# Splitting the first three hidden-layer matmul groups of token tile 0 in two along the contraction

## The chip, the cores and the metric

The kernel runs on one core of a Trainium2 chip. The metric is the time of one execution on the device, in microseconds. Every execution computes the whole reference from tensors in device memory and writes the whole output back.

## The reference

Two stages follow each other. The first is an attention over 8 batches, 8 heads, 576 positions and 64 channels, in two parts that are added; the second is a two-layer feed-forward block over 4608 tokens with an ELU between the layers.

```python
q_d, k_d, v_d = (mean over groups of 4 positions of q, k, v)      # 144 positions
out_d  = softmax(q_d @ k_d.T / 8) @ v_d                           # each row repeated 4 times
mask   = abs(pos[:, None] - pos[None, :]) < 4
out_local = softmax(where(mask, q @ k.T / 8, -1e9)) @ v
x = (repeat(out_d, 4) + out_local)        # [8*576, 8*64] = [4608, 512]
h = x @ w_in                              # w_in  [512, 2048]
g = where(h > 0, h, exp(min(h, 0)) - 1)
out = g @ w_out                           # w_out [2048, 512]
```

## The kernel before

**Pieces of work.** The attention goes batch by batch, and in a batch by pairs of heads (`j` = 0 to 3). A pair gives 128 channels of `x`, so that the four pairs are the four chunks of 128 over which the first layer's product is contracted. The feed-forward block goes by token tiles of 512 tokens (`t` = 0 to 8). Batch 0 holds tokens 0 to 575, and so all of tile 0 and the first 64 tokens of tile 1.

**Names.** Each piece is an operation with a name, an engine and a function that issues its instructions. With `b` the batch and `j` the pair: `tq`/`tk` (TensorE) turn q and k, `evq`/`evk` copy them out of PSUM, `sc` (TensorE) makes the scores, `ex` (ScalarE) is their exponential, `mask` (VectorE) applies the band where it isn't added on TensorE, `den` and `recip` give the denominators, `spr` (TensorE) and `evr` spread them, `out` (TensorE, 36 matmuls a pair) multiplies by v, `xn` (VectorE, L910 and L914) multiplies by the reciprocal, and `add` followed by batch, pair and tile (L933) adds the two parts and writes the pair's chunk of the tile buffer `xt`. In batch 0 `add000` and `add020` are GpSimd's, `add010` and `add030` VectorE's. `vc` (L572) casts a quarter of a batch's v on GpSimd after its loads `vm` on SyncE's queue have landed; `cast` (L625) casts q or k. `w0` to `w3` load quarters of `w_in`, `w4` to `w7` quarters of `w_out`, all on GpSimd's queue.

**The feed-forward block.** For tile `t` and each of 16 chunks `fc` of 128 hidden units, `mm1_t_fc` (L950) issues four matmuls of 128x512, one for each pair's chunk of `xt`, into one PSUM bank. `exp` (ScalarE, L956), `min` (VectorE, L958) and `elu` (VectorE, L961) follow; `elu` reads the bank for the last time. For each of the four groups of 128 tokens `tt`, the product with `w_out` is cut in four operations `mm2_t_tt0` to `mm2_t_tt3` (L979), each of four matmuls over four hidden chunks, in one bank; `os` (ScalarE, L995) copies it out and `st` stores it.

**What sets the order.** The program has no loop on the chip: a planner in Python writes the order out. Each operation has a rank (a due time from hand-set numbers) and an assumed duration; the planner plays the engines against each other with these, always starts the ready operation of lowest rank whose buffers are free, and keeps the order that comes out. Every engine then runs its own operations strictly in that order. A change of one operation's operands, rank or length can thus move operations that it never mentions.

**Banks.** PSUM has eight banks. While batches after the first are under way, banks 0 to 3 go to attention work in twos; banks 4 to 7 go to the first layer (`hp`, at most three at a time), the second layer (`op`, at most two) and single attention banks. Which operation gets which is settled by the planner too.

**Fillers.** Until a set time the planner puts a `fill` (L357), a matmul of 128x512 on zeros, on TensorE wherever it has nothing to do.

**Around the change.** The order on TensorE is: `spr02`, `spr03` (L841), four fills, `out02`, `out03` (L883), three fills, `tq10`, a fill, `tk10`, a fill, `mm1_0_0`, `sc10`, `tq11`, `mm1_0_1`, `tk11`, `mm1_0_2`, two fills, `sc11`, `mm1_0_3` and so on.

Of the kernel before, what the change touches and what calls it, by code (L numbers as in the profile page):

```python
# [28 lines left out]
FCN, DMC = DFF // 128, DM // 128  # L29
# [9 lines left out]
      "cast131", "vc10", "vc12")  # L39
LGATE = (None, "recip00", "evv00", "recip00", "recip02", "xn00", "xn01", "xn02", "xn03", "elu0_0", "elu0_2", "elu0_4", "elu0_8")  # L40
BY_PE = (0, 1)
WIC = (0, 512, 1024, 1536, 2048)


# [20 lines left out]
class Plan:  # L65
# [9 lines left out]
    def op(self, eng, dur, rank, fn, reads=(), writes=(), after=(), name="", nbytes=0, rate=1.0, packet=97):  # L75
        o = Op(eng, dur, rank, fn, name)
        o.nbytes, o.rate, o.packet = nbytes, rate, packet
        for b in list(reads) + list(writes):
            if b in reads or b.kind not in self.PARTS:
                o.pre.update(b.writers)  # L80
            if b not in o.bufs:
                o.bufs.append(b)
        o.pre.update(after)
        for b in writes:
            b.writers.append(o)
        for b in o.bufs:
            b.ops.append(o)
        self.ops.append(o)
        return o
# [173 lines left out]
    def emit(self):  # L263
        for o in self.order:
# [8 lines left out]
PARAM = dict(e_d0=2, e_d1=0, e_d2=0, e_d3=1, M0=27.21, P=36.34, LAG=0.71, LEAD=52.25, GAP=6.32, SC=5.0,  # L273
             DEN=30.8, OUT=1.3, OUTG=2.09, LOAD=15.53, VLOAD=34.45, VCAST=9.57, warm=3.4, FILL=36.0, WI=-28.49,
             WO=59.77, WOG=5.01, OVER=1.64, LEAD1=58.97, GAP1=6.47, OUT1=55.0, VLOAD1=29.88, LOAD1=41.47,
             CC=-34.39, tv0=-22.07, C0=-2, SC0=3.1, OUTA=-23.54, OUTB=-20, DEN0=2.92, DENB=-27.58, SPA=-26.75,
             SPB=-20.86, V0=-43, G0=0, G1=0, G2=0, G3=2, G4=12, G5=6, G6=12, G7=3, G8=13, L0=0, L1=1, L2=2,
             L3=4, L4=4, LAG0=0.75, BY4=-51.82, TV1=0.68, C1=-19.87, e_cq0=0, e_cq1=1, e_cq2=1, e_cq3=1,
             e_ck0=0, e_ck1=0, e_ck2=1, e_ck3=1, e_q0=1, e_q1=0, e_q2=0, e_q3=0, e_k0=1, e_k1=1, e_k2=0,
             e_k3=0, QG=2.5, tvA=-26, e_v0=2, e_v1=1, e_v2=2, e_v3=1, e_g0=1, e_g1=1, e_g2=1, e_g3=1, e_r0=1,  # L280
             e_r1=0, e_r2=1, e_r3=1, e_xr0=0, e_xr1=1, e_xr2=0, e_xr3=1, e_a0=1, e_a1=0, e_a2=1, e_a3=0,
# [18 lines left out]
def kernel(  # L300
# [42 lines left out]
    def at(b):  # L343
        return T[b.kind][b.slot[0]]
# [4 lines left out]
    def one(b, p0, p1, a, z):  # L349
        return PS[p0:p1, b.slot[0], a:z]  # L350

    plan = Plan(SLOTS, MOE_BANKS)
# [8 lines left out]
    op = plan.op  # L361
# [232 lines left out]
    wi_ops, wo_ops = {}, {}  # L594

    def weights(i):
        wi = i < 4
        if wi:
            lo, hi = WIC[i], WIC[i + 1]
            src = moe_w_in.rearrange("(c p) m -> p c m", p=128)[:, :, lo:hi]  # L600
# [96 lines left out]
    def pool_v(b):  # L697

        yv, zs, w = st[b], (Buf("two", b < EARLY), Buf("one")), Buf("vd")

        def tv():
            t = at(yv)
            for g in range(3):
                for i in range(4):
                    nc.tensor.matmul(  # L705
                        PS[32 * i : 32 * i + 32, zs[g // 2].slot[0] + g % 2, :], C["VR"][:],
                        t[:, :, :, 2 * g + i % 2, :], start=True, stop=True, tile_position=(0, 32 * i),
                    )

        st[b, "vd"] = w  # L710
        return yv, zs, w, tv
# [88 lines left out]
    def denominators(b, js):  # L800
# [25 lines left out]
        else:  # L826
            op("PE", 0.48, r, go, reads=list(xs.values()), writes=[z], after=[o_mark], name=f"den{b}{js[0]}").mode = "c32"
        op("DVE", 0.56, r + 0.2, lambda: nc.vector.reciprocal(out=at(c)[p0:p1], in_=one(z, p0, p1, 0, HD)),  # L828
           reads=[z], writes=[c], name=f"recip{b}{js[0]}")
        if b in BY_PE:  # L830
            if js[0] == 0:
# [72 lines left out]
    def normalize(b, j, z):  # L904
        r, y, w = out_rank(b, j), stR[b, j], Buf("xn")

        def go():
# [11 lines left out]

        op("DVE", 0.98, r + 0.2, go, reads=[z], writes=[w, y], after=[evr[b, j]] if b in BY_PE else y.writers,  # L920
           name=f"xn{b}{j}")
# [20 lines left out]
    def mm1(t, fc):  # L942
        r = M0 + P * t + P * fc / FCN
        if fc == 0:
            gts[t] = Buf("gt")
        h, e, x, gt = Buf("hp"), Buf("e"), xts[t], gts[t]

        def go(dcs):
            for dc in dcs:
                nc.tensor.matmul(  # L950
                    one(h, 0, 128, 0, TBLK), WI[:, dc, 128 * fc : 128 * fc + 128], at(x)[:, dc, :],
                    start=(dc == 0), stop=(dc == DMC - 1),
                )

        op("PE", 0.863, r, lambda: go(range(DMC)), reads=[x], writes=[h], after=[wi_ops[fc]], name=f"mm1_{t}_{fc}")
        op("ACT", 0.55, r, lambda: nc.scalar.activation(out=at(e)[:], in_=one(h, 0, 128, 0, TBLK), func=AF.Exp),  # L956
           reads=[h], writes=[e], name=f"exp{t}_{fc}")
        op("DVE", 0.42, r, lambda: nc.vector.tensor_scalar(  # L958
            out=at(e)[:], in0=at(e)[:], scalar1=1.0, scalar2=-1.0, op0=AB.min, op1=AB.add),
           reads=[e], writes=[e], name=f"min{t}_{fc}")  # L960
        op("DVE", 0.64, r, lambda: nc.vector.scalar_tensor_tensor(  # L961
            out=at(gt)[:, fc, :], in0=one(h, 0, 128, 0, TBLK), scalar=0.0, op0=AB.max, in1=at(e)[:], op1=AB.add),
           reads=[h, e], writes=[gt], name=f"elu{t}_{fc}")
# [36 lines left out]
    for b in range(B):  # L1000
# [16 lines left out]
        if b in DEN_GROUPS:  # L1017
            yv, zv, w, tv = pool_v(b)
# [9 lines left out]
    for t in range(NT):  # L1028
        for fc in range(FCN):
            mm1(t, fc)  # L1030
        for tt in range(4):
            mm2(t, tt)
# [63 lines left out]
```

## Time and profile before

| what | value |
|---|---|
| three timed runs | 349.20, 350.22, 355.65 us; median 350.22 |
| the profiled execution | 349.04 us |
| its span, first to last instruction | 347.3 us |
| TensorE busy | 331.9 us, 4672 matmuls |
| VectorE, ScalarE, GpSimd busy | 218.0, 196.4, 132.6 us |
| moved by DMA | 49.73 MB |

The profile is one execution. Its own time is 1.7 us more than its span, and 1.2 us under the median of the runs. "Idle before" is time in which an engine had nothing running, with what ended it; "issue" means that the profile shows nothing that the engine waited for. Busy time of TensorE counts matmuls of 128x512 as about 380 ns each although they start 216 ns apart when nothing is in the way, so distances between starts are used for costs.

### The profile page before, as it was taken

What the parts mean: (1) busy time and instruction counts of PE and PEld (TensorE: products, weight loads), DVE (VectorE), ACT (ScalarE), POOL (GpSimd) and SP (SyncE); (2) the same over time, 40 slices, a digit from 0 to 9 for tenths busy, and PEclk for the clock granted to TensorE, in tenths of its full rate; (3) what the DMA queues carried; (4) which work ended last, traced back from release to release, by engine and by line L of the source; (5) the groups of instructions that cost most, each with busy time, mean ns of one, the idle gap of its engine ahead of it and who ended that gap; (6) DMA issues with size and microseconds to landing.
All of it is one profiled execution on the core that took longest, in us unless ns stands there. A gap on an engine that the chain in (4) does not pass through costs nothing.

```text
span 347.3 us, 10965 instructions
## 1 busy us (share of the span) xinstructions
PE 331.9 (96%) x4672; PEld 172.4 (50%) x4672; DVE 218.0 (63%) x459; ACT 196.4 (57%) x337; POOL 132.6 (38%) x190
## 2 busy tenths in 40 slices
PE   6967999999999999899989999999999999999995
PEld 3744564555554455445544455545554444444443
DVE  6564788467474986377756786577657738655530
ACT  3582577297754686277817762776376325444431
POOL 6583133765449443732455246623410150000000
PEclk9896999999999999999999999999999999999999
DMA  8999999999999999999957995003100310001011
GB/s 204 208 213 243 195 191 205 176 192 233 223 186 202 237 227 224 178 244 216 192 131 141 189 202 137 32 32 87 64 32 30 90 64 30 32 30 60 32 54 67
DMA packets 120196, 49.73 MB, mean 143 GB/s; under 512 B 106996, under 2 KB 114708, under 8 KB 120148
## 3 DMA queue, kind: packets, MB, share of 16 engines
q1 hardware_dynamic: 112004, 39.33, 58.1%
q0 software_dynamic: 6592, 9.32, 14.5%
q8 instruction: 36, 0.59, 0.8%
q10 hardware_dynamic: 1552, 0.39, 0.6%
q14 instruction: 12, 0.10, 0.1%
HBM read 44.27 MB, written 9.55 MB: 155 GB/s over the span
## 4 chain that ended last, share of the span: by engine, by line
PE 58%; issue 0%; ACT 0%; DVE 0%; ACTq 0%
PE bank L979 27%; PE bank L950 24%; PE bank L662 2%; PE bank L883 2%; PE bank L757 1%; PE bank L705 1%; PE bank L810 1%; ACT os L995 0%; DVE xn L914 0%; ACTq L995 0%
## 5 line engine op out<-in xcount | busy, mean ns | idle before, releaser
L979 PE MATMUL bank<-WO,gt 128*128 128x512 f16 (+1 forms) x592 | 141.5, 374 | 1.5 <-DVE xn L914 1.2
L950 PE MATMUL bank<-xt,WI 128*128 128x512 f16 x576 | 141.6, 380 | 0.5 <-DVE gt L961 0.5
L956 ACT ACTIVATE e<-bank 128x512 f16<-128x512 f32 x144 | 86.8, 604 | 62.0 <-PE bank L950 45.1
L958 DVE TENSOR_SCALAR e<-e 128x512 f16<-128x512 f16 x144 | 58.0, 406 | 72.7 <-ACT e L956 72.5
L961 DVE SCALAR_TENSOR_TENSOR gt<-bank,e 128x512 f16<-128x512 f32 x144 | 98.6, 689 | 5.2
L979 PEld LDWEIGHTS <-gt 128*128 128x128 f16 x592 | 55.1, 98 | 60.4 <-DVE xn L914 1.7
L950 PEld LDWEIGHTS <-WI 128*128 128x128 f16 x576 | 53.5, 98 | 61.2 <-issue 2.9
L625 POOL CAST c<-ld 96x768 f16<-96x768 f32 x54 | 44.7, 839 | 34.5 <-issue 15.2
L933 POOL TENSOR_TENSOR xt<-xn 128x64 f16<-128x64 f16 (+7 forms) x62 | 40.4, 678 | 40.6 <-DVE xn L914 40.5
L995 ACT COPY os<-bank 128x512 f32<-128x512 f32 (+1 forms) x37 | 21.2, 575 | 40.9 <-PE bank L979 40.7
L910 DVE TENSOR_TENSOR xn<-bank,rcb 128x576 f16<-128x576 f32 x32 | 24.1, 753 | 22.0 <-POOL xt L933 9.8
L787 ACT ACTIVATE ex<-bank 128x1008 f16<-128x1008 f32 x32 | 31.6, 1010 | 8.3 <-PE bank L757 8.3
L572 POOL CAST v<-v 128x768 f16<-128x768 f32 x30 | 24.7, 848 | 23.1 <-DMA v<-in_v_dram 11.6
L677 ACT CAST qt<-bank 128x720 f16<-128x720 f32 x24 | 18.3, 763 | 18.6 <-PE bank L662 18.5
L662 PEld LDWEIGHTS <-c 96*128 96x128 f16 x288 | 18.9, 97 | 10.2 <-POOL c L625 0.5
L662 PE MATMUL bank<-ONE,c 96*128 96x120 f16 x288 | 22.1, 216 | 0.0
L855 POOL DMA_DIRECT2D rd<-rc x6 | 3.5, 579 | 47.2 <-DVE rc L828 44.7
L689 ACT CAST kt<-bank 128x576 f16<-128x576 f32 x24 | 15.8, 658 | 2.3 <-PE bank L662 2.3
L792 DVE TENSOR_TENSOR ex<-ex,MASK 128x576 f16<-128x576 f16 x28 | 14.9, 536 | 3.4 <-ACT ex L787 3.4
L883 PEld LDWEIGHTS <-v 64*64 64x64 f16 x768 | 9.4, 111 | 9.2 <-issue 9.1
L883 PE MATMUL bank<-ex,v 64*64 64x48 f16 x768 | 11.8, 191 | 1.8 <-issue 1.8
L757 PEld LDWEIGHTS <-kt 64*64 64x64 f16 x768 | 9.0, 109 | 8.0 <-issue 6.3
(90 smaller groups left out, 218.5 us busy)
## 6 DMA issues: line engine op xcount, KB each, us to landing
v<-in_v_dram SPq DMA_DIRECT2D x29, 384.0 KB, 7.7
ld<-in_q_dram SPq DMA_DIRECT2D x32, 288.0 KB, 6.0
out_dram<-os SPq DMA_DIRECT2D x35, 256.0 KB, 2.0
ld<-in_k_dram SPq DMA_DIRECT2D x28, 288.0 KB, 5.9
rcb<-rd POOLq DMA_DIRECT2D x12, 360.0 KB, 6.1
WI<-in_moe_w_in_dram POOLq DMA_DIRECT2D x4, 512.0 KB, 15.1
WO<-in_moe_w_out_dram POOLq DMA_DIRECT2D x4, 512.0 KB, 15.5
v<-in_v_dram SPq DMA_DIRECT2D x2, 368.0 KB, 8.5
```

The costliest lines, as they stand in the source:

```text
L572: f(out=at(x)[:, j].rearrange("p e c d -> p (e c) d"), in_=at(x32)[:, 12 * j : 12 * j + 12, :])
L625: f(out=at(y)[:], in_=at(x)[:].rearrange("p e c d -> p c e d"))
L662: nc.tensor.matmul(o, t[:, c, :, :], C["ONE"][:], start=True, stop=True)
L787: lambda: nc.scalar.activation(out=at(x)[:], in_=two(sc, 0, 128, 0, EW), func=AF.Exp, scale=SCALE),
L883: nc.tensor.matmul(PS[64 * e : 64 * e + 64, z.slot[0] + g, a : a + n], lhs, rhs, tile_position=(KR * r, 64 * e), **kw)
L910: nc.vector.tensor_tensor(out=_free(x, [[KB, 2], [QB, NB], [1, KB]]), in0=_free(zz, [[512 + HD, 2], *local]), in1=_free(yy, [[HB + SD, 2], ...
L933: f(out=at(xt(t))[:, j, o : o + n - a], in0=ln, in1=gn, op=AB.add)
L950: nc.tensor.matmul(one(h, 0, 128, 0, TBLK), WI[:, dc, 128 * fc : 128 * fc + 128], at(x)[:, dc, :], start=(dc == 0), stop=(dc == DMC - 1),)
L956: op("ACT", 0.55, r, lambda: nc.scalar.activation(out=at(e)[:], in_=one(h, 0, 128, 0, TBLK), func=AF.Exp), reads=[h], writes=[e], name=f"e ...
L958: op("DVE", 0.42, r, lambda: nc.vector.tensor_scalar(out=at(e)[:], in0=at(e)[:], scalar1=1.0, scalar2=-1.0, op0=AB.min, op1=AB.add), reads ...
L961: op("DVE", 0.64, r, lambda: nc.vector.scalar_tensor_tensor(out=at(gt)[:, fc, :], in0=one(h, 0, 128, 0, TBLK), scalar=0.0, op0=AB.max, in1 ...
L979: nc.tensor.matmul(one(z, 0, 128, cols.start, cols.stop), at(gt)[:, fc, 128 * tt : 128 * tt + 128], WO[:, fc, cols], start=(fc == 0), stop ...
```

## The change

For `t` = 0 and `fc` = 0, 1, 2 the operation `mm1_0_fc` becomes two. A new one, `mm1_0_fcA`, issues the matmuls of pairs 0 and 1, waits for `add000`, `add010` and the weights alone, and has a rank of its own (`PRE`, -21.0). The old name keeps the matmuls of pairs 2 and 3 and now also reads the bank. Each half has half the duration in the planner. Nothing else is edited.

```diff
+SPLIT = 3
 ...
-             L3=4, L4=4, LAG0=0.75, BY4=-51.82, ...
+             L3=4, L4=4, LAG0=0.75, PRE=-21.0, BY4=-51.82, ...
 ...
-        op("PE", 0.863, r, lambda: go(range(DMC)), reads=[x], writes=[h], after=[wi_ops[fc]], name=f"mm1_{t}_{fc}")
+        split = t == 0 and fc < SPLIT
+        if split:
+            o = Op("PE", 0.43, PARAM["PRE"] + 0.1 * fc, lambda: go((0, 1)), f"mm1_{t}_{fc}A")
+            o.pre.update(w for w in x.writers if w.name in ("add000", "add010"))
+            o.pre.add(wi_ops[fc])
+            o.bufs = [x, h]
+            for b in o.bufs:
+                b.ops.append(o)
+            h.writers.append(o)
+            plan.ops.append(o)
+        op("PE", 0.43 if split else 0.863, r, lambda: go((2, 3) if split else range(DMC)), reads=[x, h] if split else [x],
+           writes=[h], after=[wi_ops[fc]], name=f"mm1_{t}_{fc}")
```

The planner then writes other orders from this point on. On TensorE: four fills, `out02`, the three new halves, `out03`, a fill, `tq10`, two fills, `tk10`, the three old halves, `sc10`, `tq11`, a fill, `mm1_0_3`, `tk11`, five fills, `sc11`, `mm1_0_4`. The numbers of matmuls (4672) and of fills (28) are the same in both programs. Further on, three places differ most:

- VectorE does `elu0_0` before `evq11`, and `evk11` after `min0_2`; `exp0_12` (ScalarE) now stands ahead of `ex13` and `min0_12` ahead of `mask13`; in tile 1 `mask22` stands ahead of `elu1_5`, `mask23` ahead of `elu1_6`, where both stood after `elu1_7`.
- Of tile 0's second product, `mm2_0_20`, `mm2_0_21` and `mm2_0_22` stand ahead of `mm1_1_0`, and `mm2_0_23` right after `mm1_1_3`; before, the four stood after `mm1_1_2`, `mm1_1_3`, `mm1_1_5` and `mm1_1_6`. ScalarE copies that bank out (`os0_2`) after `exp1_7` in place of before it.
- GpSimd casts q and k of batch 4's first pair (`cast400`, `cast401`) ahead of `add202`, and `vc40` ahead of `add222`, `add223`, `add232`, `add233`; before, `vc40` stood behind all adds of batch 2. SyncE issues batch 4's first v loads (`vm40`, `vm40h`) ahead of the store `st0_3` and the load `load41q`, which stood ahead of them.

From the last chunks of tile 2's first product on, the orders of the two programs are the same on TensorE, and within a few operations on the other engines and queues.

## The prediction

> **What bounds the kernel now.** I read the profile's page first: how much of the span TensorE fills, and where its clock falls.
>
> ```profile
> span 347.3 us, 10965 instructions
> PE 331.9 (96%) x4672; PEld 172.4 (50%) x4672; DVE 218.0 (63%) x459; ACT 196.4 (57%) x337; POOL 132.6 (38%) x190
> ...
> PEclk9896999999999999999999999999999999999999
> ```
>
> TensorE is busy 96% of the span, so nearly every wait of TensorE goes into the time whole, and there is little idle time to win. The clock row has one low place besides the start: the fourth slice, 26 to 35 us. The waits of TensorE say why.
>
> ```profile
> PE bank L841 <- issue: 4.5, 1, 4.5
> PE bank L883 <- issue: 2.1, 4, 1.1
> ...
> PE bank L979 <- DVE xn L914: 1.2, 1, 1.2
> ```
>
> One wait of 4.5 us inside `spr03`, for nothing that the profile names; together the waits are 12 us, over half of them before 29 us. Then the timeline of TensorE behind that wait (start, length, engine, line, operation):
>
> ```profile
> 28.23 1.89 PE L357 MATMUL bank<-zero 128*128 128x512 f16 x4
> ...
> 30.56 0.51 PE L883 MATMUL bank<-ex,v 64*64 64x48 f16 x24
> ...
> 31.20 1.39 PE L357 MATMUL bank<-zero 128*128 128x512 f16 x3
> ...
> 34.12 1.03 PE L950 MATMUL bank<-xt,WI 128*128 128x512 f16 x4
> ...
> 37.85 1.04 PE L950 MATMUL bank<-xt,WI 128*128 128x512 f16 x4
> ```
>
> Fills run at half the clock (0.43 us from start to start) until about 32.4, where they go to 0.22. `out03` starts at 30.56, `mm1_0_0` at 34.12, `mm1_0_2` at 37.85. Last, the busy times by stage, to see who sets the pace where TensorE looks full (columns: stretch, length, then busy us of PE, PEld, DVE, ACT, POOL; clock, DMA share, GB/s):
>
> ```profile
> 36.00:48.00 12.00, 12.00 (x185) 6.77 (x183) 10.59 (x24) 7.80 (x13) 0.82 (x1) 1.00 1.20 192
> 48.00:60.00 12.00, 11.48 (x188) 6.00 (x187) 9.86 (x22) 8.85 (x16) 6.58 (x8) 1.00 1.19 200
> ...
> 72.00:88.00 16.00, 16.00 (x286) 8.49 (x288) 12.00 (x23) 12.47 (x22) 8.20 (x10) 1.00 1.19 214
> ```
>
> In tile 0's first product VectorE is busy 10.59 of 12 us: it paces that stage almost as much as TensorE. In tile 1's it is at 75%.
>
> **The change, part by part.** I followed the changed order of every engine with the durations of these rows: each operation starts when its engine is free and its operands and bank are there.
>
> *Up to `spr03`* the orders are the same on all engines, so the 4.5 us wait and the half clock after it stay: 0. The clock is granted again at 32.4; by the Trainium skill, TensorE: Matmul & The Clock Gate, What's actually happening, it returns after a busy window of about 3.4 us, and the trace agrees (work again from 28.1). By that section the windows run freely; a clock back at 30 would take 0.5 us off the next item.
>
> *The split itself* adds no matmul and no weight load: 3 x 4 become 3 x 2 + 3 x 2. The new halves' operands are long there: `add010` ends at 23.3 and `add000` before 25.9. They stand ahead of `out03`. Six matmuls from 30.6: four at 0.43 until 32.4, two at 0.22, so 2.2 us, by which `out03` is later (32.9). Then `xn03` (1.0) and `add030` (0.8) wait with it: that add ends at 35.1 in place of 33.66. On TensorE three fills that filled this time are gone and stand elsewhere; fill 0.22, `tq10` 0.64, two fills 0.43, `tk10` 0.64 reach 35.0. The three old halves start at 35.2 (mm1_0_0 was at 34.12) and take 6 x 0.216 = 1.3, to 36.5. All three chunks are then done 2.2 us sooner than before (37.85 + 0.87 = 38.7). This is the whole gain on offer.
>
> *What becomes of it.* The three banks of the first layer come free by `elu`. A chunk costs VectorE 0.28 to 0.49 (`min`) and 0.6 (`elu`, start to start), and beside them stand copies of 0.76 + 0.30, masks of 0.45 and reciprocals of 0.6. With VectorE at 10.59 of 12 the lead can't be kept: `evk11` now waits behind `elu0_0` and two `min`, which costs 0.8 ahead of `sc11`; `min0_12` ahead of `mask13` costs 1.0 ahead of `den12` (in the trace of before that spot waits for nothing visible; the prices are the rows of the operations passed). I reach `mm1_0_7` 0.2 us and `mm2_0_00` 0.4 us later than before (59.71). Bounds: -2.2, if the lead stays, and +1.0. I take +0.4.
>
> *Tile 1.* `mm2_0_20` to `mm2_0_22` move ahead of `mm1_1_0`. Moving 3 x 0.86 us costs nothing by itself. But they had stood between chunks of tile 1, and were what TensorE did while VectorE worked off `min` and `elu`. Around `mm1_1_3` to `mm1_1_7` it had four such pieces (3.5 us), now two. The bank of `mm2_0_2x` is also held from 67 to 87 in place of 72 to 82. With three banks for the first layer, `mm2_0_30` has to wait for `elu1_5`, which now stands behind `mask22`. The rows of ScalarE and VectorE for this chain:
>
> ```profile
> 82.77 1.91 ACT L787 ACTIVATE ex<-bank 128x1008 f16<-128x1008 f32 x2
> ...
> 83.59 0.69 DVE L961 SCALAR_TENSOR_TENSOR gt<-bank,e 128x512 f16<-128x512 f32 x1
> 84.20 1.20 DVE L792 TENSOR_TENSOR ex<-ex,MASK 128x576 f16<-128x576 f16 x2
> ```
>
> `sc23` starts at 83.1 by my count and takes 0.73; its result is seen 0.2 later; ScalarE, held by `exp1_6`, starts `ex22` at 84.5 (0.96); `mask22` 0.45; `elu1_5` 0.69: 86.5. TensorE is through with `mm1_1_7` at 84.6: a wait of 1.8 us. Smaller ones ahead of `tk22`, `mm1_1_4`, `mm1_1_5` and `sc23` add 1.2; before, this stretch waited 0.4. So +2.6, and with the 0.4 some +3. Bounds: +1 (half of the wait, if ScalarE is ahead by a little) and +4 (masks of 0.8, as the longer one of that pair beside a GpSimd cast).
>
> *Tile 2.* `vc40` now stands ahead of `add222` and `add232`, and `mm1_2_0` needs the latter. On GpSimd and on SyncE's queue before:
>
> ```profile
> 108.93 2.58 POOL L933 TENSOR_TENSOR xt<-xn 128x384 f16<-128x384 f16 x4
> ...
> 114.56 1.65 POOL L572 CAST v<-v 128x768 f16<-128x768 f32 x2 [1.51 <-DMA v<-in_v_dram]
> ```
>
> ```profile
> 101.25 3.05 SPq L997 DMA_DIRECT2D out_dram<-os  x1
> 104.41 1.25 SPq L539 DMA_DIRECT2D ld<-in_q_dram  x1
> 105.70 7.75 SPq L568 DMA_DIRECT2D v<-in_v_dram  x4
> ```
>
> `vc40` waited for its load until 114.5, after the four adds. In the new order those loads go two places sooner, past the store (3.05) and a load (1.25): about 3 us, so landed near 111.5. `xn22` and `xn23` end near 111 and 112.5 in the changed kernel. Then `vc40` to 112.3, three of the four adds (2.0) to 114.4, `mm1_2_0` at 114.6 instead of 113.2: +1.3. Bounds: 0.3 (landed sooner still) and 4.3 (landed at 114.5 as before). TensorE's stalls of 0.4 and 0.2 at `out22` (106 us) may not come back: -0.4. From there on the orders agree and TensorE has no gaps, so the difference stays.
>
> **Sum:** 0 + 0.4 + 2.6 + 1.3 - 0.4 = +3.9 us. On the profiled execution 349.04 + 3.9 = 352.9; against the median of the runs, 1.2 higher, 354.1. I give 353.5.
>
> **The rivals.**
>
> *A load sets tile 2.* The chain is mine, but `vc40` holds `add232` until 114.5 or later, or a further wait like the three "issue" waits comes (4.5, 1.1, 0.4). For it: DMA is at a share of 1.2 there, and SyncE's issues take 3 to 4 us each. Against: the loads do move up. 349.04 + 0.4 + 2.6 + 4.3 - 0.4 = 355.9, and with one more "issue" wait of 1.1 to 4.5, 357 to 360.5. The Trainium skill, Runtime: NRT & Kernel Launch, Instruction fetch mechanics, says that instructions come in blocks of 16 KiB by DMA and that this is mostly hidden; in the trace a 16,384-byte instruction transfer runs at 25.5 to 26.4, inside the 4.5 us wait, so here it isn't always.
>
> *The lead is kept (faster).* If tile 0 is paced by TensorE and not by VectorE, the 2.2 us reach the end: `mm1_0_7` would start at 42.8 in place of 45.02, and the time is 349.04 - 2.2 = 346.8. It decides if VectorE has over 2.2 us of slack between 36 and 60; the rows give 24 - 20.45 = 3.5 us idle, but 0.2 to 0.9 at a time, waiting for ScalarE.
>
> *Nothing is left of it.* The split is as designed, VectorE eats the lead, and the moved `mm2_0_2x` find their time elsewhere since `mm1_1_7` and the transposes cover VectorE: +0.4, 349.5.
>
> *The halves wait.* If `w0` lands after 30.6, PE stands in front of `out03`. Its transfer lands by 28.0 in this trace; 1 us later than 30.6 would cost 1 us, 353.9. Too near to the forecast to part from it.
>
> **How the numbers follow.** Forecast (with the last rival) 0.57, its own range 351 to 355.5; a load sets tile 2, 0.24; nothing left, 0.11; the lead is kept, 0.08. The range from 349 to 359 leaves out the lead kept and the top of the load case. Two per cent, about what a measurement of this kernel can tell from no change, is 7.0 us: 343.2 and 357.2. Slower than 357.2: most of the load case, 0.19, and 0.05 for waits in tile 1 twice as long, so 0.24. Faster than 343.2 needs the lead and the 4.5 us wait gone as well: 0.04. Within: 0.72.
>
> **What would show it right or wrong.** Right: six L950 matmuls between the two L883 groups at 30 us; the fourth hidden chunk (`mm1_0_3`) near 38 in place of 39.66, yet the first L979 at 60 and not at 57; a wait of TensorE near 85 us for L961, over 1 us; `vc40`'s L572 between the adds of L933 near 112; first L950 of tile 2 at 114 to 115 (111.47 before). Wrong: VectorE idle more than 1 us at a time between 36 and 60, no wait near 85, or a 4.5 us wait at another place than `spr03`.

## The result: slower by 1.8 and 0.4 us in two series, where 3.9 were forecast

| | kernel before | changed |
|---|---|---|
| median of the runs, first series (22 and 22) | 349.15 us | 350.75 us |
| ratio of the runs, 95% interval | 1 | 1.0052 (1.0027 to 1.0076) |
| median, second series (35 and 12) | 349.91 us | 351.62 us |
| ratio, 95% interval | 1 | 1.0012 (0.9972 to 1.0053) |
| three profiled executions, spans | 347.3, 348.3, 345.7 us | 347.9, 351.2, 351.6 us |

The medians are of all runs, while the ratios leave out those over 1.5% longer than the fastest of their kernel (two of them took 429 and 674 us, for a reason that isn't shown). The medians rise by 1.6 and 1.7 us; the ratios say +1.8 us (0.9 to 2.7) and +0.4 us (-1.0 to +1.9), so that the second series alone does not part the two kernels. The direction was forecast, the size was not: 3.9.

The first profile of the changed kernel (its own time 349.61 us), read in the prediction's order. Its page (line, then the busy us and share of the engines, then the granted clock in slices of 8.7 us):

```profile
span 347.9 us, 10964 instructions
PE 331.3 (95%) x4672; PEld 171.7 (49%) x4672; DVE 217.0 (62%) x459; ACT 196.0 (56%) x337; POOL 132.5 (38%) x190
...
PEclk9998999999999999999999999999999999999999
```

Work is the same, and so is the share. What TensorE waited for (total us, times, longest):

```profile
PE bank L842 <- issue: 2.5, 1, 2.5
PE bank L991 <- DVE xn L915: 1.5, 1, 1.5
PE bank L991 <- DVE gt L973: 1.4, 1, 1.4
...
PE bank L951 <- POOL xt L934: 0.5, 1, 0.5
```

The wait in `spr03` is 2.5 us in place of 4.5, and there are waits that the kernel before had not: 1.4 us for L973 (`elu`) and 0.5 us for L934 (`add`). The waits of 1.1 and 0.4 us for "issue" at `out40` and `out22` are gone. The timeline of TensorE around the split:

```profile
29.34 1.76 PE L951 MATMUL bank<-xt,WI 128*128 128x512 f16 x6
31.03 0.38 PE L884 MATMUL bank<-ex,v 64*64 64x48 f16 x24
...
33.38 1.46 PE L951 MATMUL bank<-xt,WI 128*128 128x512 f16 x6
...
36.26 1.02 PE L951 MATMUL bank<-xt,WI 128*128 128x512 f16 x4
```

The six matmuls of the new halves stand ahead of `out03` (31.03), the six of the old ones at 33.38, and `mm1_0_3` at 36.26 where it was at 39.66. The split does what it says. The busy times by stage (PE, PEld, DVE, ACT, POOL; clock, DMA share, GB/s):

```profile
36.00:48.00 12.00, 12.00 (x181) 6.67 (x180) 11.12 (x25) 7.93 (x15) 1.19 (x2) 1.00 1.27 198
48.00:60.00 12.00, 11.51 (x188) 6.03 (x186) 10.80 (x20) 8.61 (x15) 4.30 (x7) 1.00 1.20 194
72.00:88.00 16.00, 14.41 (x287) 7.55 (x286) 12.28 (x23) 12.63 (x23) 7.53 (x9) 1.00 1.23 208
```

VectorE is up from 10.59 to 11.12 us of 12, and TensorE has lost 1.6 of the 16 us from 72 to 88. Where:

```profile
81.36 1.95 ACT L788 ACTIVATE ex<-bank 128x1008 f16<-128x1008 f32 x2
82.43 0.46 DVE L793 TENSOR_TENSOR ex<-ex,MASK 128x576 f16<-128x576 f16 x1 [0.61 <-ACT ex L788]
82.81 0.68 DVE L973 SCALAR_TENSOR_TENSOR gt<-bank,e 128x512 f16<-128x512 f32 x1
83.54 1.02 PE L991 MATMUL bank<-WO,gt 128*128 128x512 f16 x4 [1.39 <-DVE gt L973]
```

`ex22`, `mask22`, `elu1_5`, `mm2_0_30`: the forecast's chain, link by link. And GpSimd at tile 2, with `vc40` (L573) between the adds as expected:

```profile
107.45 2.58 POOL L934 TENSOR_TENSOR xt<-xn 128x384 f16<-128x384 f16 x4
110.65 0.82 POOL L573 CAST v<-v 128x768 f16<-128x768 f32 x1 [0.62 <-DMA v<-in_v_dram]
111.44 2.59 POOL L934 TENSOR_TENSOR xt<-xn 128x384 f16<-128x384 f16 x4
```

**Where the time went, over all profiles.** One pair of profiles does not do here, since spans of one kernel differ by 2.6 and 3.7 us. So I cut each execution at the starts of four operations: `out02`, `mm2_0_00` (end of tile 0's stretch), `mm1_1_15` (tile 1), `mm1_2_15` (tile 2), and the rest up to the end of the span. The work between these marks, each operation at the shortest distance to the next that it has in any profile, is 27.3, 38.4 and 34.6 us in the kernel before and 26.5, 39.2 and 34.6 in the changed one: 0.8 us of it (`tv1`, twelve matmuls of 128x512) crosses the first border. What a stretch takes beyond its work is lost there.

| us | `out02` at | tile 0 | tile 1 | tile 2 | rest | of it waits for instructions |
|---|---|---|---|---|---|---|
| before, three profiles | 30.05, 29.24, 28.93 | 29.66, 30.15, 30.11 | 38.73, 38.83, 38.84 | 35.42, 34.97, 34.92 | 213.4, 215.1, 212.9 | 3.15, 2.59, 2.60 |
| changed, three profiles | 28.69, 28.66, 32.44 | 28.74, 29.60, 29.91 | 41.63, 41.16, 42.07 | 36.82, 39.49, 34.89 | 212.0, 212.3, 212.3 | 1.68, 2.05, 2.01 |
| mean difference | +0.5 | -0.6 | +2.8 | +2.0 | -1.6 | -0.9 |
| the same without the moved work | | +0.2 | +2.1 | +2.0 | -1.6 | |
| forecast | 0 | +0.4 | +2.6 | +0.9 | 0 | |

The orders are the same up to `out02`, so the first column is chance. Tile 0 and tile 1 came nearly as forecast. Tile 2 loses from nothing to 4.6 us. The rest, which the forecast put at nothing, is 1.6 us shorter in the mean: 0.9 us of it are waits for instructions, and the other 0.8 stand in one execution alone, the second of the kernel before (3.4 us at half the clock, behind such a wait, and one other wait of 0.6 us). The four make 2.6 us in the mean of these pairs and 0.6 where tile 2 loses nothing. The last column, the time that TensorE lost waiting for its own instructions in the rest, is what many of the experiments are about. It is counted from start to start, some 0.17 us more for each wait than the idle time that the lines print.

### The profile page after: what moved, and what is told of

The parts are those of the page before. It is cut to its first block, busy times and chain, and to the rows that moved or that the text cites. A ratio compares the mean times of both kernels' runs of the same rounds, so it can differ in the third digit from the quotient of the medians.

```text
span 347.9 us, 10964 instructions
## 1 busy us (share of the span) xinstructions
PE 331.3 (95%) x4672; PEld 171.7 (49%) x4672; DVE 217.0 (62%) x459; ACT 196.0 (56%) x337; POOL 132.5 (38%) x190
## 4 chain that ended last, share of the span: by engine, by line
PE 58%; ACT 0%; DVE 0%; issue 0%; ACTq 0%
PE bank L991 27%; PE bank L951 24%; PE bank L663 2%; PE bank L884 2%; PE bank L758 1%; PE bank L706 1%; PE bank L811 1%; ACT os L1007 0%; DVE xn L915 0%; ACTq L1007 0%
## 5 line engine op out<-in xcount | busy, mean ns | idle before, releaser
L970 DVE TENSOR_SCALAR e<-e 128x512 f16<-128x512 f16 x144 | 57.0, 399 | 72.3 <-ACT e L968 71.9
L973 DVE SCALAR_TENSOR_TENSOR gt<-bank,e 128x512 f16<-128x512 f32 x144 | 98.4, 688 | 5.2
L934 POOL TENSOR_TENSOR xt<-xn 128x64 f16<-128x64 f16 (+7 forms) x62 | 39.9, 671 | 33.0 <-DVE xn L915 32.8
L573 POOL CAST v<-v 128x768 f16<-128x768 f32 x30 | 24.6, 844 | 25.4 <-DMA v<-in_v_dram 12.8
L663 PEld LDWEIGHTS <-c 96*128 96x128 f16 x288 | 18.7, 97 | 10.9 <-issue 1.4
L793 DVE TENSOR_TENSOR ex<-ex,MASK 128x576 f16<-128x576 f16 x28 | 15.6, 556 | 3.9 <-ACT ex L788 3.8
L743 ACT CAST vd<-bank 128x512 f16<-128x512 f32 x21 | 11.6, 588 | 2.9 <-PE bank L706 2.3
```

The costliest lines, as they stand in the source:

```text
L573: f(out=at(x)[:, j].rearrange("p e c d -> p (e c) d"), in_=at(x32)[:, 12 * j : 12 * j + 12, :])
L663: nc.tensor.matmul(o, t[:, c, :, :], C["ONE"][:], start=True, stop=True)
L934: f(out=at(xt(t))[:, j, o : o + n - a], in0=ln, in1=gn, op=AB.add)
L970: op("DVE", 0.42, r, lambda: nc.vector.tensor_scalar(out=at(e)[:], in0=at(e)[:], scalar1=1.0, scalar2=-1.0, op0=AB.min, op1=AB.add), reads ...
L973: op("DVE", 0.64, r, lambda: nc.vector.scalar_tensor_tensor(out=at(gt)[:, fc, :], in0=one(h, 0, 128, 0, TBLK), scalar=0.0, op0=AB.max, in1 ...
```

## The experiments

In these kernels the order that the planner found is written out as a list for each engine, which the planner then follows, so that one part of an order can be exchanged. That moves line numbers by some 120. "Theory 1" is that the order written for tiles 1 and 2 costs more than 4 us, and that TensorE's later waits for nothing visible shrink; the rivals are given in each expectation.

**Both kernels profiled again.**

> The kernel before, profiled a second time. Theory 1 (the order written for tiles 1 and 2 costs 4 to 4.6 us, and waits of TensorE for its own instructions behind 100 us, 1.7 us in all, fall away because the work comes later against the DMA traffic): the waits named 'issue' come again at the same places, inside out40 near 175 us (about 1.1) and inside out50 near 211 us (about 0.5), and each ends 1.3 to 1.7 us after the end of a 16,384-byte instruction transfer. Rival (luck of one execution): the waits are elsewhere, or of another size by more than half, and the wait inside spr03 (4.5) and the stretch of half clock behind it (6.8 us) change too.

> The changed kernel, profiled a second time. Theory 1: no wait over 0.3 us inside out40 and out50; a wait of 1.2 to 1.6 us ahead of mm2_0_30 again, and 0.5 to 1.5 us at mm1_2_0 to mm1_2_2 for GpSimd's adds. Rival (luck): waits inside out40 or out50 as in the kernel before, and another wait inside spr03 than 2.5 us.

Spans 348.3 and 351.2 us (second entries of the table). The wait ahead of `mm2_0_30` was there again (1.4 us) and not in the kernel before; tile 2 lost 4.6 us in place of 1.9 (against the 34.9 us of the shortest executions), not at `mm1_2_0` to `mm1_2_2` as expected: 2.0 us are a wait for VectorE's `xn`, 1.7 the stretch at half the clock behind it, and 0.7 a wait for instructions at `out22`. `spr03`'s wait was 1.6 us in the kernel before and 2.6 in the changed one: it goes with the execution, not with the kernel. The waits inside `out40` and `out50` did not come again in the kernel before, and the one at `mm2_2_03` was 2.4 us in place of 1.2, so that the rival (luck of one execution) had this part right.

**The order without the split, and the split without the order.**

```diff
 # order_alone
-SPLIT = 3
+SPLIT = 0      # PE, ACT, DVE: order of before up to mm1_0_15, then that of the change;
                # POOL and SP: order of the change throughout
 # split_alone: order of before, with
- ... out02 out03 fill fill fill tq10 ...
+ ... out02 mm1_0_0A mm1_0_1A mm1_0_2A out03 tq10 ...
```

> The new order without the split: tile 0 of x unsplit and in the old order up to the last chunk of its first product, from there on every engine in the changed kernel's order. Theory 1: the loss is in the order; TensorE waits 1.4 to 1.8 us ahead of mm2_0_30 and mm1_1_8 starts 2.9 to 3.5 us later against out02 than in the kernel before; the time is 1.6 (instruction waits fall away) to 4.6 us longer, ratio 1.005 to 1.013. Rival (the loss hangs on the split halves, for instance on out03 being 2.2 us later): same time as the kernel before, ratio 0.998 to 1.002, no wait ahead of mm2_0_30.

> The split without the new order: the three new halves ahead of out03 as in the changed kernel, the three fills behind out03 left out, every engine else in the old order. Theory 1 with the tile 0 term that the two profiles show (-0.9 us): no wait ahead of mm2_0_30, ratio 0.995 to 0.999. By the forecast's own tile 0 step (lead eaten by VectorE, add030 1.5 us later): +0.4 to +1.4 us, ratio 1.001 to 1.004. Rival (the loss hangs on the halves): as the changed kernel, 1.005.

The order alone: ratio 1.0066 (1.0037 to 1.0096), which is +2.3 us, median +1.4 us. The split alone: 1.0008 (0.9962 to 1.0054), medians 349.88 and 349.84. TensorE in the order alone, at the place of the wait:

```profile
81.30 1.04 PE L1070 MATMUL bank<-xt,WI 128*128 128x512 f16 x4
83.92 1.02 PE L1110 MATMUL bank<-WO,gt 128*128 128x512 f16 x4 [1.58 <-DVE gt L1092]
```

The same wait without any split; with the split and the old order it is absent (tile 1 takes 38.96 us). The loss belongs to the order that the planner wrote, and the split itself is worth nothing that can be measured, either way (its interval reaches from -1.3 to +1.9 us).

**What are the waits for nothing visible?** In the kernel before, `out40` stands still in the middle of an operation, after 18 of its 24 matmuls:

```profile
174.59 0.32 PE L883 MATMUL bank<-ex,v 64*64 64x48 f16 x18
176.02 0.24 PE L883 MATMUL bank<-ex,v 64*64 64x48 f16 x6 [1.12 <-issue]
```

Counted from the start, the matmul at 176.02 has 2782 ahead of it. The others: 478 (`spr03`), 1758 (`out22`), 2270 (`mm2_2_03`, which the profile puts down to "DVE xn"). All are 94 more than a multiple of 128. And in both kernels the list of DMA queues (queue, packets, MB, share) has one transfer of 16,384 bytes for each 128 matmuls:

```profile
q8 instruction: 36, 0.59, 0.8%
```

In the kernel before one of them runs from 173.10 to 174.46, and TensorE goes on 1.56 us after its end. To test it, 64 small matmuls were put ahead of everything:

```diff
 # block_shift: kernel before; fills 7 to 10 become
+for _ in range(17):
+    nc.tensor.matmul(PS[:, bank, 0:16], zero[:, 0:128], zero[:, 128:144], start=True, stop=True)
```

> The kernel before, with four of its ten opening fills replaced by seventeen 16-column matmuls each: 64 more matmuls ahead of everything else, all other work and its order as before. Theory 1 (the later waits of TensorE are for its own instructions, which come in blocks of 128 matmuls): in all traces so far these waits stand at matmul 351, 478, 1758, 2270, 2782 or 3294 of TensorE's stream, all 94 or 95 more than a multiple of 128. With 64 matmuls ahead, the same places in the stream stay (94 over a multiple of 128 counted with the 64 new ones), so the operations at them are others: no wait at mm2_2_03 (139 us) and out40 (175 us), where the kernel before lost 1.2 and 1.1 us, and any new wait that nothing releases lies half a block away from the old ones. The time can fall by up to 2 us or rise by as much, by which short blocks the new places cut. Rival (the waits belong to the operations: out40 and mm2_2_03 wait for a bank or an operand that the profile doesn't name): they stay at mm2_2_03 and out40, 1 to 2 us each, whatever is ahead in the stream, and the time is that of before plus at most 1 us for the longer opening.

Where `mm2_2_03` had waited, its four matmuls and the eight behind them now run through, and a wait stands inside the next `out`:

```profile
142.11 2.77 PE L1117 MATMUL bank<-WO,gt 128*128 128x512 f16 x12
144.81 0.38 PE L1010 MATMUL bank<-ex,v 64*64 64x48 f16 x24
...
145.11 0.32 PE L1010 MATMUL bank<-ex,v 64*64 64x48 f16 x18
145.90 0.24 PE L1010 MATMUL bank<-ex,v 64*64 64x48 f16 x6 [0.47 <-issue]
```

That is matmul 2398 of this kernel, again 94 over a multiple of 128; the others stand at 351, 478, 606 and 1886 (94 or 95 over). Nothing is left at `mm2_2_03` and `out40`. So these are waits for TensorE's own instructions, and which operation pays depends on the count of matmuls ahead. The time is the same: 0.999 (0.9954 to 1.0027). The rest behind `mm1_2_15` is the shortest of all, 211.0 us with 0.6 of waits, though the queues keep their old order; but tile 0 takes 32.0 us in place of 30, with a wait of 1.2 at matmul 606 and 10.2 us at half the clock from 27 us on. The Trainium skill, Runtime: NRT & Kernel Launch, Instruction fetch mechanics, gives blocks of 16 KiB, 256 instructions, fetched while the one before runs, "mostly hidden". The block agrees (128 matmuls and 128 weight loads); hidden they are not here: the waits at 2270 and 2782 alone cost 2.3 us in the kernel before.

**Does a loss of TensorE come back?** Nine fills of 0.216 us, 1.94 us in all, ahead of one operation of the kernel before:

```diff
 # delay_150                                # delay_83
- ... mm1_3_3 mm1_3_4 ...                    - ... mm2_0_30 mm1_1_8 ...
+ ... mm1_3_3 fill x 9 mm1_3_4 ...           + ... mm2_0_30 fill x 9 mm1_1_8 ...
```

> The kernel before with nine 512-column fill matmuls (9 x 0.215 = 1.94 us of TensorE's time) ahead of mm1_3_4 (152.9 us); nothing else changes. Theory 1 (a delay of TensorE ahead of 168 us is given back in part, since the block of instructions that out40 waits for comes at a time that the DMA traffic sets, and TensorE then no longer stands still for it): out40 then starts 1.9 us later but has no wait or a shorter one (1.1 us and none in the two profiles of before, 2.2 in that of the split alone), out50 likewise (0.3 us), and the run is 0.4 to 1.2 us slower (ratio 1.001 to 1.0035). Rival (as the prediction had it: what is late there stays late to the end): 1.94 us slower, ratio 1.0056, with the waits at out40 and out50 as in the kernel before.

> The kernel before with nine 512-column fill matmuls (1.94 us of TensorE's time) ahead of mm1_1_8 (83.8 us), where the change has its wait of tile 1; nothing else. Theory 3 (a loss of TensorE there is made up for in part on the way to the end, as its waits for its own instructions and for operands that come by DMA become shorter when it is later, so that 3.65 us more of waiting for engines in two profile pairs became 1.8 us in the runs): 0.5 to 1.3 us slower, ratio 1.0015 to 1.0037. Rival (what is lost there stays lost to the end): 1.94 us slower, ratio 1.0055, and the sum of TensorE's waits behind the fills is that of the kernel before.

Ratios 1.0062 (1.0027 to 1.0097) and 1.0075 (1.0029 to 1.0121), which is +2.2 and +2.6 us: in the mean the whole 1.94, though the lower ends (0.9 and 1.0 us) don't rule out that a part came back. In the profile of delay_150 the wait at `out40` was indeed down to 0.2 us and the waits for instructions in the rest to 1.8; in that of delay_83, where TensorE comes to the rest later still, they are 2.8 us, as in the kernel before. The ratios expected by theories 1 and 3 (1.0035 and 1.0037 at most) did not come, so that TensorE's being later is not shown to shorten the rest.

**The queues.** GpSimd and SyncE by themselves: the change with their old orders, and the old kernel with their new ones.

```diff
 # queues_of_before, late_old_queues: the change; POOL and SP lists of the kernel before
 # queues_alone, queues_again, queues_third: the kernel before; POOL and SP lists of the change, e.g.
-POOL ... add202 add203 add212 add213 cast400 add222 add223 add232 add233 cast401 cast410 vc40 ...
+POOL ... cast400 cast401 add202 add203 add212 add213 vc40 add222 add223 add232 add233 ...
-SP ... load40q load40k st0_3 load41q vm40 vm40h vm42 vm42h st1_0 ...
+SP ... load40q load40k vm40 vm40h st0_3 vm42 vm42h load41q load41k ...
```

> The changed kernel, but with the orders of POOL and SP (casts, the feature-major sums, loads and stores) of the kernel before; TensorE, VectorE and ScalarE keep the order of the change. Theory 1 (tile 2's loss of 1.4 us in one profile of the changed kernel and 4.1 in the other is the order of the queues: v's cast ahead of the sums, and a value load issued between two query loads, so that a cast waited 7.5 us for a query load): mm1_1_15 to mm1_2_15 takes 35.0 to 35.4 us as in the kernel before instead of 36.8 and 39.5, tile 1's wait of 1.4 us ahead of mm2_0_30 stays, and the run is 0 to 1.5 us slower than before (ratio 1.000 to 1.004). Rival (tile 2 loses because TensorE's own order brings its groups at other times, or because a load came late by chance; the profile of the new order without the split has the new queues and no such loss): the ratio is that of the change, 1.005, and tile 2 takes 36 us or more.

> The complement of queues_of_before: the kernel before with the orders of POOL and SP taken from the change (no split, TensorE, VectorE and ScalarE as before). Theory 2 (the new order of the queues is what costs time in tile 2, TensorE's own waits of tile 1 being made up for later): mm1_1_15 to mm1_2_15 takes 36.5 us or more instead of 35.0 to 35.4, with a query or value load that a GpSimd cast waits for, and the run is 1 to 2 us slower than before, ratio 1.003 to 1.006. Rival (the loss in tile 2 is chance of the loads in any order; one profile of the old queue order has it too, 37.7 us): ratio 1.000 within 0.003.

> The kernel before with the change's order on POOL and SP, again. Theory 4 (the new order of the queues shortens TensorE's waits for instructions behind tile 2): mm1_2_15 to the end takes 212.0 to 212.5 us, though TensorE is as early as in the kernel before. Rival A (TensorE's coming later does it): 213 to 215 us as with the old queues. Either way tile 2 (mm1_1_15 to mm1_2_15) is 35 us, or up to 4 us more when a load is late. Ratio to before: 0.996 to 1.002 by theory 4 if no load is late, 1.004 as in the first runs of this kernel if loads are late in half of the executions.

> A second look at the same kernel. Theory 4: mm1_2_15 to the end 212.0 to 212.5 us again. Rival A: 213 to 215. Rival B (chance): the two looks at this kernel differ by over 1 us there.

> The changed kernel with POOL and SP as in the kernel before, again (queues_of_before gave 0.9998 with an interval of 0.0045). Theory 4: mm1_2_15 to the end takes 213 us or more, as the first time (213.3), and the ratio is 1.005 or more, since tiles 1 and 2 lose 3.2 us and nothing is given back. Rival A (TensorE's coming later shortens the waits): 212.0 to 212.5 us there, ratio 1.002 to 1.004. If the ratio is 1.000 again, neither accounts for it.

> A third look at the kernel before: mm1_2_15 to the end 213 to 215 us by theory 4 and by rival A; 212.0 to 212.5 would speak for chance. Up to mm1_2_15, counted from out02, 103.3 to 104.0 us, as in five of the six profiles with that order of TensorE (the delay of 1.94 us taken off).

> The changed kernel a third time, beside the others on one chip. If 1.8 us is its price: ratio 1.003 to 1.0075. The wait of 1.4 to 1.6 us ahead of mm2_0_30 is there; tile 2 takes 36.5 us or more if its queue order costs time in nearly every execution (theory 2), 35 to 39.5 without a rule if it is chance. TensorE's waits for other engines sum to 7.5 to 8.2 us as in both earlier profiles (3.7 and 4.9 before); its waits for instructions and the half-clock stretches are chance: 7.5 and 12.3 us in the earlier two.

The old queues under the change: 0.9998 (0.9953 to 1.0043) and 1.003 (0.9995 to 1.0065), medians +1.4 and +1.5 us. The new queues alone: 1.0042 (0.9999 to 1.0085) and 1.0073 (1.0028 to 1.0118), medians +1.5 and +1.8 us. In the profiled execution of queues_alone (672.6 us) matmuls of 128x512 started 443 ns apart throughout, in place of 216; nothing is read from it. By profile:

| us | tile 1 | tile 2 | rest | of it waits for instructions |
|---|---|---|---|---|
| change, old queues (queues_of_before, late_old_queues) | 41.76, 41.93 | 34.98, 34.83 | 213.3, 213.0 | 3.06, 2.59 |
| old order, new queues (queues_again, queues_third) | 39.23, 39.85 | 35.34, 38.16 | 211.8, 211.6 | 1.43, 1.30 |
| order_alone (new queues) | 41.27 | 34.89 | 212.1 | 1.83 |

Two things follow. First, the rest goes with the queues, not with TensorE's time: 211.6 to 212.3 us in all six profiles with the new queue order, whether TensorE is early or late; 212.9 to 215.1 in the others up to here and in the next two experiments but for two: delay_150, where it is 212.1 after taking off its 1.94 us of fills, and block_shift (211.0), where other operations pay. Theory 4 is upheld for the rest, and missed in the run times (1.0073 for the new queues where 1.004 at most was expected, 1.003 for the old ones where at least 1.005 was). In every profile, the rest without those fills, the waits for instructions, one other wait of 0.6 us in some, and half of any half-clock stretch comes to 210.2 to 210.5 us: nothing else moves there. Second, tile 2's loss isn't in every execution with the new queues. It is 1.9, 4.6 and 3.3 us in three of six and under 0.5 in three; with the old queues 2.8 in one (delay_150, where TensorE waited 2.6 us for `xn`, and `xn` 4.4 us for another late transfer, that of the denominators). In the worst (again_after), SyncE issues `load40q`, `load40k` and then the two value loads that the change brought forward:

```profile
96.84 0.37 SPq L540 DMA_DIRECT2D ld<-in_q_dram  x1
97.65 0.98 SPq L540 DMA_DIRECT2D ld<-in_k_dram  x1
98.73 9.20 SPq L569 DMA_DIRECT2D v<-in_v_dram  x2
```

and GpSimd, which has the casts of the first two (`cast400`, `cast401`) ahead of batch 2's adds in the new order, stands for them 7.5 and 0.8 us before it comes to the adds:

```profile
107.74 0.82 POOL L626 CAST c<-ld 96x768 f16<-96x768 f32 x1 [7.54 <-DMA ld<-in_q_dram]
109.32 0.82 POOL L626 CAST c<-ld 96x768 f16<-96x768 f32 x1 [0.76 <-DMA ld<-in_k_dram]
110.11 2.58 POOL L934 TENSOR_TENSOR xt<-xn 128x384 f16<-128x384 f16 x4
```

In the first profile it stood 3.0 and 2.5 us there, in queues_third 6.1 and 0.5. In order_alone `load40q` was issued 2 us sooner and `cast400` began at 102.8, and nothing was lost. In queues_again and change_again it began at 106, but there TensorE came to tile 2 some 5 us later for a slow start (`mm1_1_15` at 104.6 and 104.4 in place of 98 to 99), and little or nothing was lost either. So by these traces the two casts cost what their loads are late against TensorE; no run moved the two casts alone. change_again thus lost nothing in tile 2, and its ratio (1.0012, in the table of the result) missed the 1.003 that was expected at the least. Why such a load takes 6.6 us in one execution and 10.9 in another isn't shown.

The ratios of these kernels don't add: +0.5 us for the new order on the engines (-0.1 and +1.0), +2.0 for the new queues (1.5 and 2.6), and +1.1 for both (1.8 and 0.4), which is the change. In the profiles the new queues shorten the rest by 1.0 us under the new order of the engines and by 2.2 under the old one (1.4 without the half clock and the other wait of again_before). With intervals of 0.4% the account can't be closed further.

**The term of tile 1.**

```diff
 # mask_after_elu: as queues_of_before, and on DVE
- ... min1_5 min1_6 mask22 elu1_5 mask23 ...
+ ... min1_5 min1_6 elu1_5 mask22 mask23 ...
```

> As queues_of_before (TensorE, VectorE and ScalarE as in the change, POOL and SP as before), and on VectorE elu1_5 stands ahead of mask22 again instead of behind it; nothing else. The forecast's term for tile 1: TensorE waited 1.6 us ahead of mm2_0_30 in all four profiles with the new order, for elu1_5 behind mask22. If that chain is the cause, the wait falls to 0.5 us or less, mm2_0_00 to mm1_1_15 takes 40.0 to 40.6 us instead of 41.2 to 41.8 (and 38.8 with the old order), and the time is about 1.1 us less than queues_of_before had: ratio 0.995 to 0.9985. Rival (the wait moves to the chunk behind, since ex22 and mask22 are then late for den20, or ScalarE's exp1_5 sets elu1_5): a wait of 1 us or more stays within 5 us of that place, and the ratio stays at 0.9995 to 1.001.

```profile
81.75 1.04 PE L1070 MATMUL bank<-xt,WI 128*128 128x512 f16 x4
83.31 1.02 PE L1110 MATMUL bank<-WO,gt 128*128 128x512 f16 x4 [0.52 <-DVE gt L1092]
84.78 1.02 PE L1070 MATMUL bank<-xt,WI 128*128 128x512 f16 x4 [0.46 <-ACT os L1126]
```

The wait falls from 1.7 us to 0.5, and 0.5 us stands one place further, for `os`. Tile 1 takes 41.20 us in place of 41.76 and 41.93. So `mask22` ahead of `elu1_5` causes the wait, but undoing this link is worth 0.6 us and not 1.1: the next link is right behind, and tile 1 still takes 2.4 us more than the 38.8 of the old order, 0.8 of them moved work. The shorter stretch that was expected (40.0 to 40.6 us) and the gain in time did not come: ratio 1.000 (0.9955 to 1.0044), where queues_of_before had 0.9998.

**Tile 0's order alone.**

```diff
 # tile0_alone: SPLIT = 3; PE, ACT, DVE: order of the change up to mm1_0_15, then that of before;
 # POOL and SP as before
```

> The order and the halves of the changed kernel in tile 0 up to mm1_0_15, and from there on the order of the kernel before on all engines (POOL and SP as before throughout). Theory 1 (tile 0 gains: in the two profiles of the change, out02 to mm2_0_00 takes 28.7 and 29.6 us, in the two of before 29.7 and 30.2; the loss is all in the order behind it): 0.3 to 0.9 us faster than before, ratio 0.9975 to 0.999, and no wait ahead of mm2_0_30. Rival A (the forecast's sign: tile 0 of the change loses 0.4 us, its gain at mm1_0_3 spent on value work brought forward): ratio 1.001. Rival B (what is brought forward in tile 0 takes the place of value work that tile 1 then lacks, so tile 1 waits as in the change): ratio 1.004 to 1.006.

Ratio 1.0031 (0.9995 to 1.0067), median +0.9 us. Theory 1's gain isn't there. Up to `mm1_0_15` it took 28.5 us from `out02`, and the kernels with the old order 27.9, 28.4 and 28.4 (the three profiles of before): the halves keep nothing of their lead there. In the three profiles of the change it is 27.1, 28.0 and 28.3, so some tenths at most of the 2.2 us. (Behind that the spliced order loses 1.5 us up to `mm2_0_00` and 1.3 in tile 1, against before; that is the splice's own.)

**The part of the queues that helps, by itself.**

```diff
 # queue_tail: kernel before; SP behind load43k, POOL behind vc43 as in the change (sp_tail: SP alone)
-SP ... load43k load50q vm50 vm50h load50k st1_3 vm52 vm52h ...
+SP ... load43k vm50 load50q load50k vm50h vm52 vm52h st1_3 ...
-POOL ... cast420 cast421 cast430 spi30 spi31 ...
+POOL ... cast420 cast421 spi30 spi31 cast430 ...
```

> The kernel before, with the change's order on SP only behind load43k (from 125 us: the first value load ahead of the query load, and the two other value loads ahead of the store st1_3 instead of behind it) and on GpSimd only behind vc43 (one cast, cast430, behind spi30 and spi31). All that costs time ahead of that stays as before. Theory 4a (these loads, sooner by a few us, leave the DMA queues freer when TensorE asks for the blocks of mm2_2_03 and out40): mm1_2_15 to the end takes 212.0 to 212.4 us, the path up to there 103.3 to 104.0 from out02 as before, and the run is 1.0 to 1.7 us faster than before: ratio 0.995 to 0.997, faster than both kernels. Rival (the shortening comes from the orders ahead of 125 us, which move what the queues carry later on): 213 to 215 us and ratio 1.000.

> As queue_tail, but GpSimd keeps the order of the kernel before throughout: only the five entries of SP behind load43k are in the change's order. By theory 4a the same as queue_tail (212.0 to 212.4 us, ratio 0.995 to 0.997), since the one cast that moves on GpSimd is not waited for; if cast430's place matters, 213 us or more and ratio 1.000.

Ratios 1.0027 (0.9995 to 1.0059) and 1.001 (0.9972 to 1.0048). The waits for instructions in the rest are shorter, 1.82 and 1.64 us, as expected; but the rest takes 214.4 and 212.5 us (the other wait of 0.6 us lies in both, and in queue_tail one stretch at half the clock), and the time isn't better. Theory 4a fails where it counts. No kernel here beats the one before.

## Why the prediction was wrong, and where it held

- *Up to `spr03`: 0.* The wait of 4.5 us did not stay: 2.5, 2.6 and 0.9 us in the changed kernel, and 1.6 and 1.9 us in the other two profiles of before. It is a wait for instructions, and 4.5 was the longest seen. The prediction took one execution's luck for a property of the program.
- *Tile 0: +0.4.* Sized right, as far as three profiles tell that differ by 1.2 us there. The three chunks come early (`mm1_0_3` 36.26), VectorE fills up (11.12 of 12 us), and of the lead nothing is left at the end: +0.2 without the moved work. The sign "first L979 at 60 and not at 57" read wrong (57.43), since an earlier `out02` (by 1.36 us) and the moved 0.8 us hid it.
- *Tile 1: +2.6.* The best step. A wait of 1.8 us was forecast at 84.6 for `elu1_5` behind `mask22`; it was 1.4 us in all three profiles, from 82.2 us in the first. With the smaller ones +2.1 us. Shown by the order alone (there) and the split alone (not there). The 0.4 us that the kernel before was said to wait in this stretch aren't there: none of its three profiles has a wait over 0.1 us between `mm2_0_00` and `mm1_1_15`, and the 0.4 us of the trace stand at `out22`, which the next step took off again.
- *Tile 2: +1.3 - 0.4.* The place was right and the reason only in part. The price was worked out for `vc40`'s load, which landed in time (`vc40` waited 0.6 us). What costs is `cast400` and `cast401` ahead of the adds, a move that I had listed and not priced: 0 to 4.6 us, mean 2.0, by when their loads land (of the 4.6, 1.7 are half clock behind the wait and 0.7 a wait for instructions). The first L950 of tile 2 started at 112.27, not at 114 to 115, and waited 0.5 us behind its first group. Nor do the prediction's own times add up: 111.47 + 0.4 + 2.6 - 0.4 is 114.1, and its 114.6 is then a price of 0.5 us for this step, where it reckoned 1.3 from a place of 113.2 that these terms don't give. That SyncE's issues take 3 to 4 us holds for two of the lines around it (3.05 and 3.72), not for the value loads (7.75 for four). The bounds of 0.3 and 4.3 were about right, though for another load. The -0.4 at `out22` was chance: again_after waited 0.55 us there.
- *"From there on the orders agree and TensorE has no gaps, so the difference stays": 0.* **This is the step that failed.** TensorE has gaps there: 2.6 to 3.2 us of waits for instructions in the kernel before, 1.7 to 2.1 in the changed one, and a half-clock stretch in one profile. The rest is 1.6 us shorter (213.8 to 212.2 in the mean), 0.9 by these waits and 0.8 by what one profile of the kernel before has besides, which is chance as far as three profiles tell. The prediction had the evidence: "issue" four times, one of 1.1 us at 176 us, and a wait of 1.2 us put down to `xn`. And "the orders agree" was true of TensorE but not of the queues, which is where the difference was: the same rest came with the new queues under the old TensorE order. That is shown in profiles; in run time, the new queues alone were slower (+1.5 and +2.6 us) and the tail of the queues' order alone gained nothing that could be measured, so what part of the new queues' order shortens the rest, and how far that enters the median, stays open.

Of the rivals, "a load sets tile 2" describes again_after (though it was another load), and "nothing is left of it" describes tile 0. That the loss is one of the order and not of the split, which neither put as a question, is the clearest result.

## What to carry to other kernels

A kernel whose order a planner writes is changed wherever the planner's order changes: compare the whole order on every engine and queue first, and price the edit itself last. When a sum says "no gaps from here on, so it stays", look for waits that have no releaser behind that point; if they stand a constant number of instructions apart, as here by 128 matmuls, count them: matmuls put ahead will show whether the engine waits for its own instructions. One profile gave the place of tile 1's loss, the same in all, but not the size of a loss that a load or such a wait sets: take three.

## What the runs showed of the chip

- TensorE's waits for instructions stand 128 matmuls or a multiple of that apart, where a block of 16,384 bytes is late. In 19 profiles (all but that of queues_alone), the transfers that TensorE then waited for over 0.15 us between 40 and 182 us started 1.8 to 6.8 us (median 5.1) after it had entered the block ahead, took 1.0 to 1.5 us, and TensorE went on 1.3 to 1.8 us after their end; the waits were up to 2.9 us. For the blocks without such a wait the median start is 1.8 us. A short block is not enough: one of 5.8 us ahead of 88.2 us in the kernel before ends without a wait. Why some of these transfers start late isn't shown. In all 19 TensorE waited at matmuls 351 and 478, ahead of tile 0. In the three profiles of before it lost 8.9, 6.4 and 5.3 us to such waits.
- The clock is granted at half for stretches that are multiples of 3.41 us: 3.4 to 23.9 us in all ahead of 40 us, differing between executions of one program. Later such a stretch came behind stalls of 2.0 us (113.6 to 117.0 in again_after), 2.4 (again_before) and 1.6 (delay_83 and queue_tail), and not behind ones of 2.5 and 2.9 at the same place (queues_of_before, tile0_alone). Here is the first of them (PE, PEld, DVE, ACT, POOL; clock):

```profile
110.00:120.00 10.00, 7.97 (x108) 3.96 (x106) 3.26 (x8) 4.06 (x8) 9.16 (x14) 0.83 1.25 202
```

  The Trainium skill, TensorE: Matmul & The Clock Gate, What's actually happening, has windows of 3.4 us that run freely, and a clock that falls after an idle one. The lengths of the stretches agree; but here stalls of 1.6 to 2.4 us, shorter than a window, were enough in four executions, and two longer ones were not.
